# A fused attention and mixture-of-experts kernel: GpSimd's subtraction in two pieces, one group of routing operations a step later, a lower bound on one column at a time

## The chip, the cores and the metric

One core of a Trainium2 chip runs the whole program. The engines are TensorE (PE, with its weight loads PEld), VectorE (DVE), ScalarE (ACT), GpSimd (POOL) and SyncE (SP, which here issues most DMAs). The metric is device time in microseconds, the median of repeated runs.

## The reference, cut to what matters

```python
def _attn_ref(q, kv, w_sr):                      # B=4, C=128, q: 4 x 12288 x 128
    kv_pool = kv.reshape(B, H // r, r, W // r, r, C).mean(axis=(2, 4))
    k = v = kv_pool.reshape(B, -1, C) @ w_sr     # 768 keys per batch
    s = scale * (q @ k.transpose(0, 2, 1))
    a = np.exp(s - s.max(-1, keepdims=True))
    a /= a.sum(-1, keepdims=True) + 1e-09
    return a @ v
def _moe_ref(x, w_gate, w_output_gate, w1, w2):  # 8 experts, 49152 tokens x 128, hidden 1024
    logits = x @ w_gate
    e_idx = np.argmax(logits, axis=1)
    probs = np.exp(logits - logits.max(-1, keepdims=True))
    probs /= probs.sum(-1, keepdims=True) + 1e-09
    gate_w = probs[np.arange(N), e_idx]
    eom = 1.0 / (1.0 + np.exp(-(x @ w_output_gate)))
    ...
        h = np.maximum(x[mask] @ w1[e], 0.0)
        out[mask] = gate_w[mask, None] * eom[mask, e, None] * (h @ w2[e])
```

## The kernel before, in words

Values of 32 bits are carried as two halves of 16 bits, a high one (rounded) and a low one (the rest), and a product is three matmuls: high by high, high by low, low by high.

The queries are cut into 96 groups of 512 tokens (index `i`), each into four blocks of 128 (index `j`). The main loop runs over `i` and eight steps `s`; every second step starts a block. For each block, `qk` makes the scores S (six matmuls of 384 columns, L483 to L487) and DVE their negative maximum `nm` (L489, L490). `qk_exp` lets ACT write the probabilities `pr`, 768 columns of float32 (L504), and afterwards lets DVE scale a finished piece of output `o` (L825). `qk_round` lets ACT write the high half of the probabilities into `ph` (L517), and POOL the low half, `pr` minus the high half (L518). A DMA of SP transposes `ph` into `PT`. `pr` has two buffers, `ph` three.

A group later, `pv` multiplies PT with the values (18 matmuls, L540) into U, whose halves ACT (L544) and DVE (L545) write; two groups later, `moe_h` and `moe_y` push it through the one expert picked for the batch from the mean of its keys: per slice of the hidden layer three matmuls H (L790 to L792), the high half HH by ACT (L795), the low half HL by DVE (L796), and four slices later three matmuls Y (L805 to L807). PE's order is written out by hand, so PE stops where an operand is late.

Every four groups make a unit, and `routing` finds each token's expert, gate and place in the lists of tokens that go elsewhere. It is a Python generator whose pieces, between its `yield`s, are issued one or two per step between the work above; nearly all run on DVE on small tiles: L611 to L617; L620 to L626; L630 to L637 (`oh`, one where a token's expert is); then `se` (L656) and the output gate of the chosen expert, `zz` = gates times choice, summed to `z` and scaled (L658 to L661); the exponential of `z` (L663, ACT); the count of tokens `cnt` (L667), for which two small matmuls must have run; L669 to L676; L681; L684 to L687; L690 to L696. Then POOL scatters the rows to the lists by 16 indirect DMAs (L705). The last units are marked `ending`; there nothing is moved.

Beside this, each batch's keys and values are prepared during the batch before: POOL adds the pooled rows (L296 to L300), PE transposes them (L304), and `largest` (L170, L171) bounds the maximum found by DVE from below, for keys (`ve`) and for weights (`wm`, two columns).

`LAG` is 2: groups 0 and 1 run before the expert's work begins. The order within one engine is the order in which these calls are made.

Of the kernel before, what the change touches and what calls it, by code (L numbers as in the profile page):

```python
# [26 lines left out]
ALU = mybir.AluOpType  # L27
# [3 lines left out]
ts = bass.ts  # L31
# [6 lines left out]
NK = 768  # L38
# [11 lines left out]
LAG = 2  # L50
# [4 lines left out]
class Cfg:  # L55
# [24 lines left out]
    WA = ((6, 0, (0, 0)), (9, 0, (1, 0, 0)), (11, 0, (2, 0, 0), (1, 0, 1)), (13, 0, (2, 0, 1), (0, 1)),  # L80
          (16, 0, (1, 1, 0)), (18, 0, (2, 1, 0), (1, 1, 1)), (20, 0, (2, 1, 1)))
    PRB = 2
    QL, QT, QN = 0, 3, 6
    QLA = ((7,), (7,)) + ((0, 3, 6),) * 6
    QP1 = 5
# [15 lines left out]
def body(ctx, tc, q, kv, w_sr, w_gate, w_og, w1, w2, out, cfg=Cfg):  # L101
    nc = tc.nc
    pe, act, dve, pool, sp = nc.tensor, nc.scalar, nc.vector, nc.gpsimd, nc.sync
# [64 lines left out]
    def largest(m, ps):  # L168

        dve.tensor_reduce(out=m, in_=ps, op=ALU.max, axis=AX.X)  # L170
        dve.scalar_tensor_tensor(m, m, 2.0 ** -100, m, op0=ALU.max, op1=ALU.max)  # L171

    def powers(lo, inv, m):

# [10 lines left out]
    gps = psH.tile([P, GT], F32, tag="H", name="gps")  # L185
    pe.transpose(gps[:, 0:P], gmb, ident)
    largest(g3[:, 1:2], gps[:, 0:P])
    powers(g3[:, 2:3], g3[:, 3:4], g3[:, 1:2])
    dve.memset(wgB, 0.0)
# [41 lines left out]
    def kv_prep(b, fast):  # L231
# [99 lines left out]
        if fast:  # L331
            mean()
            choice(ps[:, 1, 0:E])
            next(QP[1])
            warm(cfg.WM[1])
        largest(e2[:, 5:6], ps[:, 0, 0:P])
        powers(e2[:, 0:1], e2[:, 1:2], e2[:, 5:6])
        dve.tensor_scalar(e2[:, 2:3], e2[:, 1:2], 2.0 ** 14, None, op0=ALU.mult)
# [159 lines left out]
    def qk_exp(i, j):  # L498

        S, nm, es, scale = QX.pop((i, j))  # L500
        c, g = unit[i]
        pr = wk.tile([P, NK], F32, tag="pr", bufs=cfg.PRB, name=f"pr{i}_{j}")
        bl = g * GB + j
# [6 lines left out]
    def qk_round(i, j):  # L510

        pr = PR.pop((i, j))
        ph = wk.tile([P, 2, NK], F16, tag="ph", bufs=3, name=f"ph{i}_{j}")
        if j in cfg.PHD and i < LAG:
            dve.tensor_copy(ph[:, 0, :], pr)
        else:
            act.activation(ph[:, 0, :], pr, AF.Copy)  # L517
        pool.tensor_tensor(ph[:, 1, :], pr, ph[:, 0, :], op=ALU.subtract)  # L518
        PH[(i, j)] = (ph, None, now[0])


# [72 lines left out]
    def routing(c):  # L594
# [8 lines left out]
        def T(nm, n=1, dt=F32, bufs=1):  # L603
            return rt.tile([P, CB * n], dt, tag=nm, bufs=bufs, name=f"{nm}{c}")[:, 0:nb * n]

        def T3(nm, n=E, bufs=1):
            return T(nm, n, F32, bufs).rearrange("p (b e) -> p b e", e=n)
# [38 lines left out]
        ending = g0 + ng + 2 >= NG  # L646
# [7 lines left out]
            hooks.append((now[0] + 1, counts))  # L654
        se = T("se")
        dve.tensor_reduce(out=se, in_=dn, op=ALU.add, axis=AX.X)  # L656
        zz = T3("dn")
        dve.tensor_tensor(zz, L[:, :, E:2 * E], oh, op=ALU.mult)  # L658
        z = T("z")
# [20 lines left out]
        x = T("x0", E)  # L680
# [44 lines left out]
    def w_split(b, t):  # L725
# [25 lines left out]
        if b:  # L751
            hooks.append((T, turn))
            while not ps:
                yield
            yield
            largest(m[:, 0:2], ps[0][:, :, 384:512])
        else:
            yield from until(0)
            wps = psY.tile([P, GT], F32, tag="Y", name="wmp")
            for n in range(2):  # L760
                pe.transpose(wps[:, ts(n, P)], mb[:, n, :], ident)
            largest(m[:, 0:2], wps[:, 0:2 * P].rearrange("p (n x) -> p n x", n=2))
# [223 lines left out]
    with tc.manual_schedule(engines={pool.engine, sp.engine, pe.engine, act.engine, dve.engine}):  # L986
# [30 lines left out]
        def k0(i):  # L1017
            return cfg.KV0[min(i // GPB, 1)]
# [6 lines left out]
        def after_values(ri, rc):  # L1025
            if rc is not None:
                logits(rc)

                def turn():
                    logits_turn(rc)  # L1030
                    rts.append([routing(rc), 0, rc])
                at(cfg.RG, turn)
            n = max(0, 8 * cfg.UD + cfg.UDS * ri - now[0])
            at(cfg.UT + n, u_turn, ri)
            at(cfg.UO + n, u_out, ri)
# [34 lines left out]
        for i in range(NG + OL):  # L1070
# [5 lines left out]
            for s in range(8):  # L1076
# [11 lines left out]
                for o in cfg.ORD if mi >= 0 else cfg.ORDA:  # L1088
# [4 lines left out]
                    if o == "s" and att and s % 2 == 0:  # L1093
                        qk(i, s // 2)
                        while late:
                            qk_round(*late.pop(0))
                    if o == "x" and att and s % 2 == 0:
                        qk_exp(i, s // 2)
                    if o == "r" and att and s % 2:
                        if s // 2 in cfg.PHD and i < LAG:  # L1100
                            late.append((i, s // 2))
                        else:
                            qk_round(i, s // 2)
# [7 lines left out]
                    if o == "u":  # L1111
                        for d, h in cfg.PVA:
                            x = i - d // 8
# [35 lines left out]
                if att and s == cfg.QL:  # L1149
                    n = min(ql + 2, i + cfg.QN + 1, NG)  # L1150
# [7 lines left out]
                if kp:  # L1158
                    n = (8 * (i % GPB - k0(i)) + s) % cfg.KVP[min(i // GPB, 1)]
# [25 lines left out]
        while events:  # L1185
            i, s = divmod(min(events), 8)
# [39 lines left out]
```

## Time and profile before

| | |
|---|---|
| median of 3 runs | 1962.98 us (1962.57 to 1963.02) |
| the profiled execution's own time | 1944.66 us |
| its span, first to last instruction | 1942.9 us |
| busy: PE, DVE, ACT, POOL | 96%, 77%, 68%, 60% |
| mean granted PE clock | 0.993 |

Busy shares are averages over the span. A busy PE is shown with modelled ends: its matmuls overlap, so a wait of PE is shown shorter than it is.

### The profile page before, as it was taken

What the parts mean: (1) busy time and instruction counts of PE and PEld (TensorE: products, weight loads), DVE (VectorE), ACT (ScalarE), POOL (GpSimd) and SP (SyncE); (2) the same over time, 40 slices, a digit from 0 to 9 for tenths busy, and PEclk for the clock granted to TensorE, in tenths of its full rate; (3) what the DMA queues carried; (4) which work ended last, traced back from release to release, by engine and by line L of the source; (5) the groups of instructions that cost most, each with busy time, mean ns of one, the idle gap of its engine ahead of it and who ended that gap; (6) DMA issues with size and microseconds to landing.
All of it is one profiled execution on the core that took longest, in us unless ns stands there. A gap on an engine that the chain in (4) does not pass through costs nothing. (4 is left out here: it accounts for less than half of the span.)

```text
span 1942.9 us, 31028 instructions
## 1 busy us (share of the span) xinstructions
PE 1870.8 (96%) x10225; PEld 951.0 (49%) x10225; DVE 1504.7 (77%) x3005; ACT 1321.3 (68%) x2391; POOL 1159.8 (60%) x996
## 2 busy tenths in 40 slices
PE   6999999999999999999999999999999999999997
PEld 4444455454445544545444554444445555545544
DVE  6776877888878778788787787787877877877773
ACT  3767767676776766676767776667677767767653
POOL 2537566564675676754756656656466456466462
PEclk9999999999999999999999999999999999999999
DMA  8877788788988887878788988778778778786642
GB/s 234 161 153 160 168 163 180 153 163 169 183 170 165 170 178 159 168 145 187 141 168 172 187 174 169 162 155 151 167 148 167 152 147 166 154 159 142 133 105 70
DMA packets 884017, 311.63 MB, mean 160 GB/s; under 512 B 827584, under 2 KB 833857, under 8 KB 883856
## 3 DMA queue, kind: packets, MB, share of 16 engines
q1 hardware_dynamic: 870944, 309.18, 78.7%
q0 software_dynamic: 12480, 0.40, 0.5%
q8 instruction: 81, 1.33, 0.3%
q14 instruction: 80, 0.66, 0.1%
q10 hardware_dynamic: 432, 0.07, 0.0%
HBM read 56.83 MB, written 51.25 MB: 56 GB/s over the span
## 5 line engine op out<-in xcount | busy, mean ns | idle before, releaser
L518 POOL TENSOR_TENSOR ph<-pr,ph 128x768 f16<-128x768 f32 x384 | 633.0, 1649 | 629.5 <-ACT ph L517 383.2
L796 DVE SCALAR_TENSOR_TENSOR HL<-H,HH 128x512 f16<-128x512 f32 x768 | 526.0, 686 | 142.3 <-ACT HH L795 127.9
L795 ACT ACTIVATE HH<-H 128x512 f16<-128x512 f32 x768 | 456.5, 594 | 246.6 <-PE H L792 240.3
L504 ACT ACTIVATE pr<-S,nm,qm 128x768 f32<-128x768 f32 x384 | 381.0, 992 | 240.2 <-DVE nm L490 222.7
L705 POOL DMA_INDIRECT scr<-rw,idx x384 | 383.1, 998 | 95.8 <-issue 88.1
L489 DVE TENSOR_REDUCE nm<-S 128x1 f32<-128x768 f32 x384 | 365.3, 951 | 86.8 <-PE S L487 86.3
L540 PE MATMUL U<-PT,V 128*128 128x512 f16 (+1 forms) x1746 | 406.1, 378 | 7.4 <-DVE HL L796 5.1
L517 ACT ACTIVATE ph<-pr 128x768 f16<-128x768 f32 x380 | 319.9, 842 | 2.4 <-DMA PT<-ph 1.9
L790 PE MATMUL H<-U,w 128*128 128x512 f16 x768 | 292.3, 381 | 12.3 <-DVE HL L796 7.0
L791 PE MATMUL H<-U,w 128*128 128x512 f16 x768 | 292.1, 380 | 0.0
L807 PE MATMUL Y<-HL,w 128*128 128x512 f16 x768 | 291.3, 379 | 0.7 <-DVE HL L796 0.6
L792 PE MATMUL H<-U,w 128*128 128x512 f16 x768 | 291.7, 380 | 0.0
L805 PE MATMUL Y<-HH,w 128*128 128x512 f16 x768 | 291.4, 379 | 0.3 <-ACT ys L810 0.3
L806 PE MATMUL Y<-HH,w 128*128 128x512 f16 x768 | 291.3, 379 | 0.0
L540 PEld LDWEIGHTS <-V 128*128 128x128 f16 x1746 | 171.4, 98 | 212.6 <-issue 11.5
L483 PE MATMUL S<-K,qT 128*128 128x384 f16 x768 | 189.2, 328 | 13.1 <-ACT pr L504 7.5
L487 PE MATMUL S<-K,qT 128*128 128x384 f16 x768 | 189.0, 328 | 1.3 <-DVE qT L459 1.0
L485 PE MATMUL S<-K,qT 128*128 128x384 f16 x768 | 188.9, 328 | 0.5 <-DVE K L349 0.5
L825 DVE TENSOR_TENSOR o<-S,msw 128x256 f32<-128x256 f32 x176 | 74.8, 425 | 89.0 <-ACT pr L504 87.6
L792 PEld LDWEIGHTS <-w 128*128 128x128 f16 x768 | 75.3, 98 | 91.4 <-issue 1.4
L807 PEld LDWEIGHTS <-w 128*128 128x128 f16 x768 | 75.2, 98 | 90.8 <-issue 0.3
L805 PEld LDWEIGHTS <-w 128*128 128x128 f16 x768 | 75.2, 98 | 88.3 <-issue 0.5
(209 smaller groups left out, 1865.4 us busy)
## 6 DMA issues: line engine op xcount, KB each, us to landing
kvs<-in_kv_dram SPq DMA_DIRECT2D x96, 256.0 KB
q<-in_q_dram SPq DMA_DIRECT2D x96, 256.0 KB
urows<-uT SPq DMA_DIRECT2D x96, 256.0 KB
out_dram<-o SPq DMA_DIRECT2D x96, 256.0 KB
PT<-ph SPq DMA_TRANSPOSE x384
scr<-rw,idx POOLq DMA_INDIRECT x384
wr<-in_moe_w_dram SPq DMA_DIRECT2D x8, 512.0 KB
tw<-in_moe_w_dram SPq DMA_DIRECT2D x4, 512.0 KB
```

The lines of the kernel that those rows point to most:

```text
L489: dve.tensor_reduce(out=nm[:, 0:1], in_=S[:, :, 0:384], op=ALU.max, axis=AX.XY, negate=True)
L504: act.activation(pr.rearrange("p (a k) -> p a k", a=2), S[:, :, 0:384], AF.Exp, bias=nm[:, 1:2], scale=es, accum_out=SUMS[c][:, bl:bl + 1])
L517: act.activation(ph[:, 0, :], pr, AF.Copy)
L518: pool.tensor_tensor(ph[:, 1, :], pr, ph[:, 0, :], op=ALU.subtract)
L540: pe.matmul(PVP[i][:, cols], ops[n][0], ops[n][1][:, cols], start=(n == 0), stop=(n == len(ops) - 1))
L705: ins = pool.indirect_dma_start(out=scr, out_offset=bass.IndirectOffsetOnAxis(ap=idx[:, bl:bl + 1], axis=0), in_=rw[:, bl, :], in_offset=None,
L790: pe.matmul(H, w1h[:, ts(f, P)], UH, start=True, stop=False)
L792: pe.matmul(H, w1l[:, ts(f, P)], UH, start=False, stop=True)
L795: act.activation(HH, H, AF.Relu)
L796: dve.scalar_tensor_tensor(HL, H, 0.0, HH, op0=ALU.max, op1=ALU.subtract)
L805: pe.matmul(Y, w2h[:, ts(f, P)], HH, start=(f == 0), stop=False)
L807: pe.matmul(Y, w2h[:, ts(f, P)], HL, start=False, stop=(f == NFB - 1))
```

## The change

Three edits. `qk_round`, from group 2 on, issues POOL's subtraction as two operations of 384 columns in place of one of 768. `routing` yields once more, between `se` and `zz`, except in the ending units. `largest` bounds each column of `m` by an operation with a constant (`tensor_scalar`), where one operation read `m` twice (`scalar_tensor_tensor`).

```diff
+    PLN = 2
...
         dve.tensor_reduce(out=m, in_=ps, op=ALU.max, axis=AX.X)
-        dve.scalar_tensor_tensor(m, m, 2.0 ** -100, m, op0=ALU.max, op1=ALU.max)
+        for n in range(m.shape[1]):
+            dve.tensor_scalar(m[:, n:n + 1], m[:, n:n + 1], 2.0 ** -100, None, op0=ALU.max)
...
             act.activation(ph[:, 0, :], pr, AF.Copy)
-        pool.tensor_tensor(ph[:, 1, :], pr, ph[:, 0, :], op=ALU.subtract)
+        for x in [slice(0, NK)] if i < LAG else [ts(h, NK // cfg.PLN) for h in range(cfg.PLN)]:
+            pool.tensor_tensor(ph[:, 1, x], pr[:, x], ph[:, 0, x], op=ALU.subtract)
...
         dve.tensor_reduce(out=se, in_=dn, op=ALU.add, axis=AX.X)
+        if not ending:
+            yield
         zz = T3("dn")
         dve.tensor_tensor(zz, L[:, :, E:2 * E], oh, op=ALU.mult)
```

On DVE, this is the order of the second unit's routing around the new `yield`, before (`dn` is the tile that `zz` lies in, `nm` the scores' maximum, `o` the output, `U` the low half of U):

```order
L656 TENSOR_REDUCE se_2285<-dn_2262 128x16
L658 TENSOR_TENSOR dn_2287<-L_2210,oh_2269 128x128
L660 TENSOR_REDUCE z_2289<-dn_2287 128x16
L661 TENSOR_TENSOR z_2289<-z_2289,rinv_2214 128x16
L489 TENSOR_REDUCE nm_3_2313<-S_3_2304 128x1
L490 TENSOR_SCALAR nm_3_2313<-nm_3_2313,qm_860 128x1
L796 SCALAR_TENSOR_TENSOR HL_4_2321<-H_4_2316,HH_4_2320 128x512
L825 TENSOR_TENSOR o_2229<-S_3_2304,msw_1468 128x256
L545 SCALAR_TENSOR_TENSOR U_2343<-U_2292,U_2343 128x512
L796 SCALAR_TENSOR_TENSOR HL_5_2353<-H_5_2348,HH_5_2352 128x512
L489 TENSOR_REDUCE nm_0_2375<-S_0_2366 128x1
```

And the same place of the changed kernel, whose lines are numbered a little higher:

```order
L659 TENSOR_REDUCE se_2317<-dn_2293 128x16
L491 TENSOR_REDUCE nm_3_2340<-S_3_2331 128x1
L492 TENSOR_SCALAR nm_3_2340<-nm_3_2340,qm_867 128x1
L801 SCALAR_TENSOR_TENSOR HL_4_2348<-H_4_2343,HH_4_2347 128x512
L830 TENSOR_TENSOR o_2260<-S_3_2331,msw_1524 128x256
L548 SCALAR_TENSOR_TENSOR U_2370<-U_2319,U_2370 128x512
L663 TENSOR_TENSOR dn_2374<-L_2240,oh_2300 128x128
L665 TENSOR_REDUCE z_2376<-dn_2374 128x16
L666 TENSOR_TENSOR z_2376<-z_2376,rinv_2244 128x16
L801 SCALAR_TENSOR_TENSOR HL_5_2384<-H_5_2379,HH_5_2383 128x512
L491 TENSOR_REDUCE nm_0_2407<-S_0_2398 128x1
```

The three operations of `zz` and `z` went from ahead of `nm`, HL, `o` and the low half of U to behind them, ahead of the next HL and `nm`; what follows (`cnt` and so on) keeps its place, since the generator waited a step for the count's matmuls anyway. Only in the first unit do later pieces shift too. ACT's exponential of `z` moves from behind U's high half to behind the next block's probabilities. PE's and SP's orders are the same in both kernels.

On POOL, five rows in the middle of the first batch, before (`scr` are the scatters):

```order
L518 TENSOR_TENSOR ph_2_2748<-pr_2_2729,ph_2_2748 128x768
L705 DMA scr<-rw_2583,idx_2578 394240x4 x2
L518 TENSOR_TENSOR ph_3_2819<-pr_3_2785,ph_3_2819 128x768
L705 DMA scr<-rw_2583,idx_2578 394240x4 x2
L518 TENSOR_TENSOR ph_0_2869<-pr_0_2849,ph_0_2869 128x768
```

And with the change:

```order
L521 TENSOR_TENSOR ph_2_2787<-pr_2_2768,ph_2_2787 128x384 x2
L710 DMA scr<-rw_2619,idx_2614 394240x4 x2
L521 TENSOR_TENSOR ph_3_2859<-pr_3_2825,ph_3_2859 128x384 x2
L710 DMA scr<-rw_2619,idx_2614 394240x4 x2
L521 TENSOR_TENSOR ph_0_2910<-pr_0_2890,ph_0_2910 128x384 x2
```

Each subtraction became two in a row (376 of the 384), with nothing of POOL between them; the order is otherwise kept, but for the first unit, where two additions and a scatter change places with their neighbours.

## Rows read from the trace of the kernel before

**Rows 1.** Steady stretch: us, busy of PE, PEld, DVE, ACT, POOL, clock, DMA.

```profile
150.00:1880.00 1730.00, 1695.81 (x9280) 854.40 (x9278) 1367.26 (x2674) 1209.41 (x2184) 1078.15 (x919) 1.00 0.82 162
```

**Rows 2.** Waits, whole run: waiting engine and line, releaser, us in total, times, longest.

```profile
PE H L790 <- DVE HL L796: 7.0, 12, 1.3
...
PE U L540 <- DVE HL L796: 5.1, 6, 1.7
...
PE H L790 <- DVE U L545: 4.7, 11, 1.0
...
ACT pr L504 <- POOL ph L518: 2.0, 4, 0.7
```

**Rows 3.** DVE by line, 150 to 1880 us: busy us, mean ns, idle before.

```profile
L658 DVE TENSOR_TENSOR dn<-L,oh 128x128 f32<-128x128 f32 (+1 forms) x23 | 34.1, 1482 | 0.8
...
L634 DVE TENSOR_TENSOR oh<-t,m 128x128 f32<-128x128 f32 (+1 forms) x23 | 8.6, 375 | 0.8
```

**Rows 4.** Timeline of the third unit's `zz`: start us, us, engine, line, [idle before].

```profile
283.02 2.11 PE L540 MATMUL U<-PT,V 128*128 128x512 f16 x9
...
283.82 1.63 POOL L518 TENSOR_TENSOR ph<-pr,ph 128x768 f16<-128x768 f32 x1 [3.66 <-ACT ph L517]
283.89 1.79 DVE L658 TENSOR_TENSOR dn<-L,oh 128x128 f32<-128x128 f32 x1
...
286.04 0.18 DVE L661 TENSOR_TENSOR z<-z,rinv 128x16 f32<-128x16 f32 x1
...
289.03 0.69 DVE L545 SCALAR_TENSOR_TENSOR U<-U,U 128x512 f16<-128x512 f32 x1
...
289.77 0.38 PE L790 MATMUL H<-U,w 128*128 128x512 f16 x1 [0.34 <-DVE U L545]
...
290.45 1.64 POOL L518 TENSOR_TENSOR ph<-pr,ph 128x768 f16<-128x768 f32 x1 [5.00 <-ACT ph L517]
```

**Rows 5.** PE busy from 2 to 7 us behind each L658, 22 stretches.

```profile
sum 110.00, PE 104.52; mean PE 4.75
```

**Rows 6.** Timeline around 533 us, POOL's operations back to back.

```profile
532.57 1.07 DVE L684 SCALAR_TENSOR_TENSOR st<-cnt,ebase 128x8 f32<-128x8 f32 x1
...
533.57 1.26 POOL L296 TENSOR_TENSOR kvs<-kvs 128x512 f32<-128x512 f32 x1
```

**Rows 7.** PE busy in six stretches at other routing pieces, from 371 to 1005 us.

```profile
sum 30.00, PE 24.63; mean PE 4.10
```

**Rows 8.** Timeline around 1400 us: a bound of two columns.

```profile
1397.64 1.38 DVE L171 SCALAR_TENSOR_TENSOR wm<-wm 128x2 f32<-128x2 f32 x1
```

**Rows 9.** PE busy, 932 to 938 and 1397.6 to 1403.6 us, behind such bounds.

```profile
sum 12.00, PE 8.82; mean PE 4.41
```

**Rows 10.** Timeline around 448 us.

```profile
447.56 1.64 POOL L518 TENSOR_TENSOR ph<-pr,ph 128x768 f16<-128x768 f32 x1 [1.86 <-ACT ph L517]
...
447.98 0.15 DVE L265 TENSOR_SCALAR chi<-ch 128x1 int32<-128x1 f32 x1
```

**Rows 11.** Two stretches, columns as in rows 1.

```profile
771.00:775.00 4.00, 1.15 (x6) 0.39 (x5) 2.79 (x5) 3.28 (x9) 2.35 (x3) 1.00 0.85 202
775.00:778.50 3.50, 3.50 (x11) 1.87 (x12) 0.92 (x1) 1.91 (x4) 3.12 (x3) 0.51 0.99 213
```

**Rows 12.** POOL by line and shape, whole run, columns as in rows 3.

```profile
L518 POOL TENSOR_TENSOR ph<-pr,ph 128x768 f16<-128x768 f32 x384 | 633.0, 1649 | 629.5 <-ACT ph L517 383.2 <-issue 220.4 <-DVE ph L515 21.2
...
L778 POOL TENSOR_TENSOR w<-wr,w 128x512 f16<-128x512 f32 x16 | 18.6, 1164 | 1.1 <-ACT w L774 1.0
```

**Rows 13.** PE busy, 20 stretches of 4 us behind L690 to L696 (0.82 us).

```profile
sum 80.00, PE 77.45; mean PE 3.87
```

**Rows 14.** Timeline around 926 us: L692 beside a subtraction.

```profile
926.09 1.64 POOL L518 TENSOR_TENSOR ph<-pr,ph 128x768 f16<-128x768 f32 x1 [4.79 <-issue]
926.18 1.59 DVE L692 SCALAR_TENSOR_TENSOR idx<-sel,ix 128x16 int32<-128x16 f32 x1
...
929.87 0.38 PE L790 MATMUL H<-U,w 128*128 128x512 f16 x1 [1.28 <-DVE HL L796]
```

## The prediction

> **What bounds the kernel now.** I read the busy time of the steady stretch first, then who waits for whom, then the timeline around a few of those waits. In the stretch from 150 to 1880 us PE is busy for 1695.8 of 1730 us at full clock, while DVE is idle for a fifth of it and POOL for more than a third [rows 1]. PE bounds it; only the 34 us in which PE waits can be won, and somewhat more, since a matmul of 512 columns is shown 0.38 us long and started every (2.11 - 0.38) / 8 = 0.216 us [rows 4]: each wait is really 0.16 us longer than shown. PE waits mostly for DVE: 16.8 us in 29 waits for HL and for the low half of U [rows 2].
>
> Why is DVE late, with so much idle time? `zz` (L658) takes 1482 ns on average; `oh` (L634), the same shape with two operands from SBUF, takes 375 ns [rows 3]. The timeline shows the reason: POOL's subtraction began at 283.82, `zz` at 283.89, and `zz` ended at 285.68, 0.23 us behind the subtraction's end [rows 4]. L684, of 8 columns, was held the same way, and so was the bound L171, of two [rows 6, 8]. A DVE operation with two inputs from SBUF that starts while POOL computes stands still until POOL's operation ends; I call it caught. Not every operation is: HL reads one input from PSUM, and `tensor_scalar` on one column took its usual 0.15 us in the middle of a subtraction [rows 10]. Behind a caught operation all of DVE's queue is late (`nm`, HL, `o`, U), then ACT, then PE: at 289.77 PE waited for U, whose DVE part had queued behind that `zz` [rows 4].
>
> **The change part by part.** The sum is made against the profiled execution (1944.7 us, of which 1942.9 are span); it lies 18.3 us below the median of the runs, 1963.0, and I take the same microseconds off the median.
>
> *`zz` a step later.* In 22 steady units `zz` starts beside a subtraction and loses 1.48 - 0.38 = 1.1 us, with everything of DVE behind it. In the five microseconds that begin 2 us after each, PE idles 110.0 - 104.5 = 5.5 us; these are some 20 waits, so really 5.5 + 20 x 0.16 = 8.7 us [rows 5]. Now `nm`, HL, `o` and U go first. The group stands behind U and ahead of the next HL; its other two operations ended 0.54 us behind `zz` (286.22 against 285.68, rows 4), so not caught it takes 0.38 + 0.54 = 0.92 us. L690 to L696 (0.82 us) stand in just such a place already, behind U: in 20 stretches behind them PE idles 2.55 us [rows 13], and 17 of the 20 show no idle time; the rest has the key transposition in it. So a group of this length is covered there by PE's queued matmuls. I take three quarters of the 8.7 as won, 6.5 us; bounds 0 and 8.7.
>
> Can it be caught again? `zz` itself starts with U's end, `z` times `rinv` (L661, two inputs from SBUF) 0.38 + 0.36 = 0.74 us after (286.04 against 285.68, rows 4). The next subtraction started 0.73 us after U's end (290.45 against 289.72, rows 4), and will start a little earlier, since ACT's exponential of `z` has left the place between. That is a dead heat. Caught by a piece, it loses at most the piece, 0.9 us, ahead of HL and `nm`. I put 1.0 us against all units; bounds 0 and, at the one wait of 1.28 + 0.16 us seen behind a caught operation in this very place [rows 14], 22 x 1.44 = 31.7.
>
> *Two pieces.* 768 columns take 1649 ns and 512 take 1164 [rows 12]: 1.9 ns a column and some 0.19 us fixed. A piece of 384 should take 0.92 us and a pair 1.84, so POOL works 376 x 0.19 = 73 us more. What hides it: POOL waits 383 us for ACT in front of this line alone [rows 12], and ACT waited for a subtraction to free `pr` only 4 times, 2.0 us in all [rows 2]. I cost it at nothing. If a piece took as long as 512 columns, the pair would take 2.33 us, 256 us more in all, still less than that idle time; without the cover each block would pay its 0.19 us, 73 us. What the pieces give: DVE is let in between POOL operations that stand back to back. L684 ended at 533.64 although POOL's next had begun at 533.57 [rows 6]. So a caught operation waits for the end of a piece, on average half as long. In six stretches where other routing pieces were caught PE idles 5.4 us, in 6 waits, really 6.3 [rows 7]. Half of it, 3.2 us; bounds 0 (some were caught by key additions of 512 columns, which stay whole) and 6.3.
>
> *The bound.* L171 was held for 1.38 us [rows 8]; two `tensor_scalar` on one column take 2 x 0.15 by the one that ran beside a subtraction [rows 10]. That is 1.1 us earlier for what queues behind it, twice where PE stopped: 12.0 - 8.8 = 3.2 us idle in four waits, really 3.8 [rows 9]. I take 3.0; bounds 0 and 3.8.
>
> A rule speaks against this edit. The Trainium skill's page "VectorE: DVE Perf Modes", section "The perf-mode tier table", gives fp32 `tensor_scalar` in SBUF a two-port mode, and its page "SBUF — State Buffer", section "SBUF: two separate sides", says that an operation in such a mode fights GpSimd for one port pair as one with two SBUF inputs does. By that the bound would be caught as before and the sum 3.0 us smaller. The rows on one column say otherwise, and I go by them.
>
> *The clock.* At 771 PE idles 2.85 us, then runs 3.4 us at a granted clock of 0.51, the lower of its two levels (1.2 GHz) [rows 11]. Much the same happens once more, at 1236 us. DVE's lateness from earlier caught pieces adds to both, and key preparation does too. I take 2.0 us of the some 9 that both cost (2 x 2.85 idle and 2 x 1.7 of clock); bounds 0 and 9.
>
> Sum: -6.5 + 1.0 - 3.2 - 3.0 - 2.0 = -13.7 us: 1931 for a profiled execution, 1949 for the median.
>
> **The rivals.**
>
> *Caught again.* `z` times `rinv` starts just behind the first piece in nearly all units. It loses some 0.7 us of DVE there, where `zz` lost 1.1 and cost PE 8.7 / 22 = 0.4 us a unit; at 0.3 a unit it gives back 6.6 us in place of the 1.0: 1955. For it: the dead heat. Against: L690 to L696 show room for 0.82 us there [rows 13].
>
> *All of it.* The waits that follow from caught operations vanish, the two falls of the clock too: 8.7 + 6.3 + 3.8 + 9 = 28: 1935. Against: the key preparation, which stays.
>
> *PE waits elsewhere.* DVE is on time, and ACT's chain (probabilities, then HH, then `ph`) ends as late as before: PE loses elsewhere most of what it wins, and 3 us remain: 1960. For it: ACT works for 1209 of 1730 us [rows 1] and has its own order. Against: ACT had waited for the late `nm`.
>
> *Slower: the second piece follows before DVE gets in.* A caught operation then waits for 1.84 us, more than the 1.65 before, and `z` times `rinv` is caught ahead of HL. With 1.44 us of PE as in [rows 14] in half of the units that is +15.8, with +1 for the other pieces, against -8.7 and -3.0: +5, 1968. It decides from about 8 caught units on. Against: L684 was let in between two operations [rows 6]. The same page "SBUF — State Buffer" of the Trainium skill says that whoever starts first holds the port pair for the whole instruction; it does not say who is next, and the trace agrees as far as it goes.
>
> **How the numbers follow.** The forecast 0.56 (its own range 1943 to 1957, from taking half or nearly all of each term), caught again 0.17, all of it 0.09, elsewhere 0.12, slower 0.06. Within 0.2% (4 us) is about what a measurement of this kernel cannot tell from no change, so slower starts at 1967. Faster gets nearly all of the first three, 0.79; same gets the fourth and the edges of its neighbours, 0.14; slower 0.07. The range reaches from the all-of-it case to the elsewhere case with its margin: 1935 to 1963.
>
> **What would show it.** Right: `zz` near 0.38 us on average and no idle time of PE from U's low half behind it; L684 near 0.5 us; the bounds at 0.15 us; pieces near 0.92 us and POOL some 70 us busier; PE idle in the steady stretch near 22 us instead of 34. Wrong: `z` times `rinv` near 1 us on average (caught again); DVE operations ending behind a second piece (not let in); ACT waiting for POOL at L504, or pieces above 1.2 us (the cover gone); or PE's idle time unchanged under other names.

## The result, and the profile after

The changed kernel took 1943.28 us (median of 4 runs, 1942.22 to 1944.98) beside 1962.83 for the kernel before (4 runs): 19.6 us less, a ratio of 0.9901 with a 95% interval of 0.9884 to 0.9918. In a later series, on another chip, the same pair took 1927.21 and 1942.17: 15.0 us less, 0.9925 (0.9911 to 0.9939). The forecast was 14 us less, 1949 beside 1963, a ratio of 0.9930: it lies inside the second interval and 0.0012 above the end of the first.

The profiled execution of after (1944.02 us, one of its timed runs) is only 0.6 us shorter than that of before (1944.66). Two rows of each timeline show why: ACT's copies of the expert's finished sums, `ys`, of group 3 and of group 91, groups 0 to 95 (columns: start us, us, engine, line). Before:

```profile
143.50 0.59 ACT L810 ACTIVATE ys<-Y 128x512 f32<-128x512 f32 x1
...
1879.50 0.59 ACT L810 ACTIVATE ys<-Y 128x512 f32<-128x512 f32 x1
```

After:

```profile
140.16 0.59 ACT L815 ACTIVATE ys<-Y 128x512 f32<-128x512 f32 x1
...
1865.75 0.59 ACT L815 ACTIVATE ys<-Y 128x512 f32<-128x512 f32 x1
```

After is 3.3 us ahead at group 3 and 13.75 at group 91. It loses nearly all of that again in the last groups. This is its timeline there:

```profile
1876.51 0.38 PE L797 MATMUL H<-U,w 128*128 128x512 f16 x1
...
1879.05 0.38 PE L797 MATMUL H<-U,w 128*128 128x512 f16 x1
...
1884.78 0.60 ACT L800 ACTIVATE HH<-H 128x512 f16<-128x512 f32 x1 [7.16 <-remote]
...
1888.35 0.60 ACT L800 ACTIVATE HH<-H 128x512 f16<-128x512 f32 x1 [2.96 <-remote]
...
1890.42 1.11 PE L842 MATMUL ot<-ident,ys 128*128 128x128 f32 x4 [10.99 <-ACT ys L815]
```

ACT writes the HH at 1888.35 from the H that PE had finished at 1876.89; in between ACT does almost nothing, and PE, which is at the end of its own queue, idles 10.99 us. The releaser is given as "remote": by the ends shown, nothing was late. The ends of matmuls are modelled, though, and the trace also records when the semaphore changed by which H tells ACT that it is done: here at 1884.76 and 1888.32, each 0.02 us ahead of an HH, and 9.2 and 11.4 us behind the ends shown for these two H. So ACT started when it was told; late was the signal, or the true end of the matmul. The experiments below say whether this stall belongs to the change.

In the steady stretch the rows answer to [rows 1 to 3]. First the busy times of 150 to 1860 us (columns as in [rows 1]; up to 1860, since the stall of after begins ahead of 1880), before and after:

```profile
150.00:1860.00 1710.00, 1676.12 (x9176) 844.72 (x9174) 1352.02 (x2626) 1201.20 (x2167) 1068.50 (x906) 1.00 0.82 163
```

```profile
150.00:1860.00 1710.00, 1682.06 (x9231) 850.25 (x9229) 1343.09 (x2651) 1211.67 (x2175) 1128.46 (x1270) 1.00 0.82 163
```

PE idles 27.9 us in place of 33.9. In the second traces of the two kernels, below, it is 24.4 and 37.9 us.

Then DVE by line in after, 150 to 1880 us (busy us, mean ns, idle before):

```profile
L440 DVE SCALAR_TENSOR_TENSOR q<-q,qm,q 128x512 f16<-128x512 f32 x87 | 81.2, 934 | 0.0
...
L666 DVE TENSOR_TENSOR z<-z,rinv 128x16 f32<-128x16 f32 (+2 forms) x24 | 11.4, 475 | 0.8
...
L663 DVE TENSOR_TENSOR dn<-L,oh 128x128 f32<-128x128 f32 (+2 forms) x24 | 9.2, 383 | 0.1
...
L689 DVE SCALAR_TENSOR_TENSOR st<-cnt,ebase 128x8 f32<-128x8 f32 x24 | 8.1, 337 | 0.0
```

`zz`, now L663, takes 383 ns where it took 1482 [rows 3]: caught in one unit only (0.82 us at 207 us), no longer in all 22. `z` times `rinv` (L666) takes 475, far above the 0.18 us of one that is not caught [rows 4]: caught in part of the units. L684, now L689, takes 0.34 us. The waits of PE and ACT in after, whole run (total us, times, longest):

```profile
PE H L795 <- DVE HL L801: 4.9, 6, 1.3
...
PE S L485 <- DVE cnt L672: 3.4, 2, 2.1
...
PE U L543 <- DVE HL L801: 2.5, 4, 1.2
...
ACT pr L506 <- POOL ph L521: 2.3, 4, 1.0
...
PE H L795 <- DVE U L548: 1.3, 2, 1.0
```

PE's waits for HL and U's low half fell from 16.8 us in 29 [rows 2] to 8.7 us in 12, and ACT waits for a subtraction as seldom as before.

### The profile page after: what moved, and what is told of

Same layout as the page of the kernel before. It is cut to its first block, busy times and chain, and to the rows that moved or that the text cites. A ratio compares the mean times of both kernels' runs of the same rounds, so it can differ in the third digit from the quotient of the medians.

```text
span 1942.3 us, 31545 instructions
## 1 busy us (share of the span) xinstructions
PE 1867.1 (96%) x10225; PEld 952.2 (49%) x10225; DVE 1485.9 (76%) x3009; ACT 1328.2 (68%) x2391; POOL 1216.9 (63%) x1372
## 5 line engine op out<-in xcount | busy, mean ns | idle before, releaser
L521 POOL TENSOR_TENSOR ph<-pr,ph 128x384 f16<-128x384 f32 (+1 forms) x760 | 686.0, 926 | 559.2 <-issue 440.0
L710 POOL DMA_INDIRECT scr<-rw,idx x384 | 387.8, 1010 | 94.9 <-issue 90.9
```

The lines of the kernel that those rows point to most:

```text
L521: pool.tensor_tensor(ph[:, 1, x], pr[:, x], ph[:, 0, x], op=ALU.subtract)
L710: ins = pool.indirect_dma_start(out=scr, out_offset=bass.IndirectOffsetOnAxis(ap=idx[:, bl:bl + 1], axis=0), in_=rw[:, bl, :], in_offset=None,
```

## The experiments

**The kernel before again, and each edit alone (four kernels beside each other).** The first is unchanged:

> The kernel before, unchanged. The profiled execution of before (1944.7 us) was 18.3 us shorter than its timed runs (1962.8), while the one of after (1944.0 us) is one of its timed runs, and 13.6 us of it are one stall of PE at 1877 to 1890 us, where before shows none. Theory A: the stall near the end comes and goes from run to run or from kernel to kernel, whatever the three edits do; then this trace shows a stall of 10 us or more near the end and its time is 1958 to 1963 us, or it shows none and the time is near 1945. Theory B: the 18.3 us of before are spread over the steady stretch (PE idle there 45 us or more in place of 34); then the change wins in its timed runs more than the traces show.

It took 1959.63 us against 1959.59. Its group 91 stands here:

```profile
1883.34 0.59 ACT L810 ACTIVATE ys<-Y 128x512 f32<-128x512 f32 x1
```

That is 3.8 us behind the first trace of before, and from there to the end of the span it takes 1957.9 - 1883.3 = 74.6 us where the first trace took 1942.9 - 1879.5 = 63.4. Together 15.0 us, all of the difference between the two executions (1959.64 - 1944.66). The 11.2 us lie where after has its stall: HH starts at 1900.82 for an H that is shown to end at 1893.18 (its signal stands at 1900.80), and PE idles 8.6 us. So theory A holds: this stall is no work of the change; before has it too, in an execution as long as its timed runs. Theory B falls: PE idles 37.9 us in 150 to 1860, not 45.

The step alone:

```diff
         dve.tensor_reduce(out=se, in_=dn, op=ALU.add, axis=AX.X)
+        if not ending:
+            yield
         zz = T3("dn")
```

> Before with the one yield between se and zz and nothing else. Prediction's step: zz is no longer caught, minus 6.5 us (0 to 8.7), and z times rinv caught in some units gives back 1.0 (0 to 6.6), so 1955 to 1958 us. Rival, pieces carry the gain: z times rinv is caught by the whole subtraction of 1.65 us in about half of the units and nothing is won, 1962 us. Rival, the gain is the end stall only: 1943 to 1946 or 1962, and nothing in between.

It took 1951.94 us, ratio 0.9964 (0.9951 to 0.9977): by the ratio 7 us less (4.5 to 9.6). The expected 1955 to 1958, meant from 1963, are 5 to 8 less, so this fits. The five microseconds at `zz`'s old place, 2 to 7 us behind the end of `se`, in 22 units as in [rows 5] (which had 5.48 us idle), now show 0.43:

```profile
sum 110.00, PE 109.57 PEld 54.33 DVE 93.17 ACT 66.95 POOL 42.95; mean PE 4.98 PEld 2.47 DVE 4.24 ACT 3.04 POOL 1.95
```

`z` times `rinv` is caught by the whole subtraction in 11 of 22 units, 842 ns on average, and still nearly all of the gain stays. The rival "nothing is won" fell.

The pieces alone:

```diff
-        pool.tensor_tensor(ph[:, 1, :], pr, ph[:, 0, :], op=ALU.subtract)
+        for x in [slice(0, NK)] if i < LAG else [ts(h, NK // cfg.PLN) for h in range(cfg.PLN)]:
+            pool.tensor_tensor(ph[:, 1, x], pr[:, x], ph[:, 0, x], op=ALU.subtract)
```

> Before with the subtraction in two pieces and nothing else. Prediction's step: caught operations wait half as long, minus 3.2 us for the other pieces (0 to 6.3) and some 0.5 to 0.7 us of each zz, 22 units, another 4: 1955 to 1960 us; zz falls from 1.48 to about 0.9 us. Rival, the second piece follows before DVE gets in: zz rises to 1.8 us or more and the time is 1963 to 1970. Rival, the end stall only: 1943 to 1946 or 1962, nothing in between.

It took 1950.23 us, ratio 0.9956 (0.9943 to 0.9969), by the ratio 8.6 us less, where 3 to 8 were expected. `zz` takes 750 ns and is caught in every unit as before, but by a piece:

```profile
L660 DVE TENSOR_TENSOR dn<-L,oh 128x128 f32<-128x128 f32 (+2 forms) x24 | 18.0, 750 | 0.8
```

At its place PE now idles 110.0 - 107.4 = 2.6 us in place of 5.48:

```profile
sum 110.00, PE 107.40 PEld 52.63 DVE 91.85 ACT 79.78 POOL 29.20; mean PE 4.88 PEld 2.39 DVE 4.17 ACT 3.63 POOL 1.33
```

So at this place the pieces alone take half of what the step takes.

The bounds alone:

```diff
-        dve.scalar_tensor_tensor(m, m, 2.0 ** -100, m, op0=ALU.max, op1=ALU.max)
+        for n in range(m.shape[1]):
+            dve.tensor_scalar(m[:, n:n + 1], m[:, n:n + 1], 2.0 ** -100, None, op0=ALU.max)
```

> Before with the two or one one-column bounds and nothing else. Prediction's step: minus 3.0 us (0 to 3.8), 1959 to 1963 us, each bound 0.15 us. Rival, by the rule that two-port modes fight for the port too: the bounds that meet a subtraction take 1 us or more and the time does not change, 1963. Rival, the end stall only: 1943 to 1946 or 1962, nothing in between.

It took 1956.15 us, ratio 0.9988 (0.9980 to 0.9997): by the ratio 2.3 us less, between 0.6 and 3.9. The timeline shows a pair of bounds that starts 0.27 us into a whole subtraction and takes 0.21 us:

```profile
1395.00 1.63 POOL L519 TENSOR_TENSOR ph<-pr,ph 128x768 f16<-128x768 f32 x1 [1.47 <-ACT ph L518]
1395.27 0.21 DVE L172 TENSOR_SCALAR wm<-wm 128x1 f32<-128x1 f32 x2
```

The rival, taken from a rule, falls with that. None of the three times lies at 1943 to 1946 or at 1962, as the rival of all three had it, so the end stall does not carry the gain either.

**After again, without the step, with four pieces, and with ACT's stream shifted (four kernels on another chip, before 1942.17 us there).**

> The kernel after, unchanged, beside the kernel before on one chip, to stand next to the parts. If the parts add up (0.36, 0.44 and 0.12 per cent alone), 0.991 of before or 18 us less; if the step and the pieces win the same waits twice, the parts alone would give more than the whole and the ratio would be 0.993 to 0.994. The stall near the end, in ACT's HH of slices 731 to 733 and 743 to 746, which all traces show but the first of before, should be there again with 12 to 14 us.

Measured 1927.21 us, 0.9925 (0.9911 to 0.9939), between the two expectations. The stall was not there. The timeline shows HH behind H at once, and the transposition `ot` without a wait:

```profile
1872.13 0.38 PE L797 MATMUL H<-U,w 128*128 128x512 f16 x1
...
1872.54 0.60 ACT L800 ACTIVATE HH<-H 128x512 f16<-128x512 f32 x1 [0.70 <-PE H L797]
...
1873.84 0.66 PE L842 MATMUL ot<-ident,ys 128*128 128x128 f32 x4
```

Group 91 stands at 1861.38, and from there it takes 63.3 us, as in the first trace of before. The stall thus comes with the series a kernel is run in, not with the kernel: 11 to 13 us in after and in the four kernels above, where before took 1963 and 1960 us beside them, none in this trace, where it took 1942. By these times the runs of before have it where those of the other kernel have it, so it should cancel in each ratio; the runs without a trace cannot show it.

The yield taken out of after:

```diff
         dve.tensor_reduce(out=se, in_=dn, op=ALU.add, axis=AX.X)
-        if not ending:
-            yield
         zz = T3("dn")
```

> After without the yield: pieces and bounds. With pieces alone zz was still caught 23 times but for 0.42 us in place of 1.16, and the waits of PE in the 5 us behind it fell from 11.2 to 4.0 us. Theory, overlap: the step can only win those 4.0, less 1.5 that z times rinv gives back ahead of the count's wait, so this kernel is 2 to 4 us slower than after. Rival, additive: the step is worth its 7.7 us also beside the pieces; this kernel is 6 to 8 us slower than after.

Measured 1928.91 us, 0.9929 (0.9915 to 0.9942): 1.7 us slower than after by the medians and 0.8 by the ratios, which the runs do not tell from nothing; the additive rival, 6 to 8, falls. Alone the step won 7 us, beside the pieces 1 or 2 (up to 3 by the spread of the six runs of each). So they win, for the most part, the same waits.

Four pieces:

```diff
-    PLN = 2
+    PLN = 4
```

> After with four pieces of 192 columns in place of two of 384. A piece should take 0.19 + 192 x 0.0019 = 0.55 us, four 2.2 us, POOL 143 us more busy than in after. Theory, a caught operation waits for the end of the piece that it meets: z times rinv loses 0.3 us in place of 0.65, all caught operations of DVE together some 40 us in place of 53, and PE wins 1 to 4 us, 1940 to 1943. Rival, the cover is gone: ACT waits for POOL at the probabilities and the low halves come late, slower than after by 2 us or more. Rival, PE covers what is left of the catches: the same as after within 1 us.

Measured 1921.95 us, 0.9896 (0.9880 to 0.9912): 5.3 us faster than after, a little more than the 1 to 4 expected. The reason given was only half right. `z` times `rinv` fell to 316 ns on average, but all catches of DVE together did not shrink: L440 rose from 934 to 1064 ns, though the pieces are shorter.

```profile
L440 DVE SCALAR_TENSOR_TENSOR q<-q,qm,q 128x512 f16<-128x512 f32 x87 | 92.6, 1064 | 0.0
```

PE's waits for HL and U's low half are 5.4 us there, where the trace of after beside it has 9.6, and PE runs one stretch at the lower clock in the steady stretch where after has two; what each of these is worth is not separated. POOL's row, with a piece of 0.56 us, gives 1504 x 0.561 = 844 us by the means, and 789 us busy, as back-to-back pieces overlap a little:

```profile
L521 POOL TENSOR_TENSOR ph<-pr,ph 128x192 f16<-128x192 f32 x1504 | 789.3, 561 | 412.5 <-issue 335.1 <-ACT ph L519 70.4 <-POOL ph L521 2.1
```

ACT's copies ahead of everything:

```diff
+        dm = cst.tile([P, 64], F32, name="dm")
+        dve.memset(dm[:, 0:1], 0.0)
+        for n in range(1, 41):
+            act.activation(dm[:, n:n + 1], dm[:, 0:1], AF.Copy)
         ld, vprep = kv_load(0, True), kv_prep(0, True)
```

> After with 40 small copies on ACT ahead of everything, where ACT idles until 10 us (plus one memset on DVE). It asks what the stall near the end is tied to: ACT ran HH of slices 731 to 733 and 743 to 746 of the hidden layer 2 to 11 us after its operands were there, the same slices in five traces. Theory, ACT's place in its instruction stream: the stall moves some 40 instructions forward, to slices of about 705 to 722, or goes, and the time changes by several us up to 13. Rival, tied to the work there (the scatters of the last units, what ACT waits for): the same slices, the same 12 to 14 us, the time of after within 2 us.

Measured 1926.71 us, the time of after within 0.5. Since no kernel of this series had the stall, it says nothing about its cause: inconclusive.

**Going on: is the step needed, do other pieces help, and how small is too small (three kernels beside each other, before 1943.82 us).** Four pieces without the yield:

> Four pieces and the bounds, without the yield (after has two pieces, the bounds and the yield). If pieces and step win the same waits, zz caught by a piece of 0.55 us loses 0.2 to 0.3 us only and the step has nothing left to win: the ratio to before is that of four pieces with the step, 0.9896, within 0.001. Rival, the step is worth something of its own (2 us or more beside two pieces, the interval of the runs left that open): 0.9905 to 0.992.

Measured 1922.36 us, 0.9898 (0.9883 to 0.9912): the same as four pieces with the step, so the step has nothing left to win there that these runs can tell (some 4 us between two series). `zz` is then caught in its old place but takes 432 ns, 0.06 more than uncaught:

```profile
L661 DVE TENSOR_TENSOR dn<-L,oh 128x128 f32<-128x128 f32 (+2 forms) x24 | 10.4, 432 | 0.8
```

Four pieces with the other long operations of POOL halved (on top of the edit above):

```diff
-                pool.tensor_tensor(x[:, 0, :], x[:, 0, :], v, op=ALU.add)
+                for p in (slice(0, 256), slice(256, 512)):
+                    pool.tensor_tensor(x[:, 0, p], x[:, 0, p], v[:, p], op=ALU.add)
...
-            pool.tensor_tensor(ws[n][:, 1, ts(x, 512)], t[:, n, ts(x, 512)], ws[n][:, 0, ts(x, 512)], op=ALU.subtract)
+            for p in (2 * x, 2 * x + 1):
+                pool.tensor_tensor(ws[n][:, 1, ts(p, 256)], t[:, n, ts(p, 256)], ws[n][:, 0, ts(p, 256)], op=ALU.subtract)
```

> Four pieces with the step and the bounds, and the other long operations of POOL in two pieces too: the key additions (54 of 512 columns, 1.30 us) and the low halves of the weights (16, 1.16 us), 0.7 us each piece. Theory, what is caught waits for the end of the operation that it meets, so the catches by these (0.5 to 1.2 us, some 20 in a run) halve and PE wins 1 to 3 us more: 0.988 to 0.989 of before. Rival, PE does not wait behind these catches any more: 0.9896 as with four pieces alone.

Measured 1917.15 us, 0.9869 (0.9855 to 0.9884), the fastest of all: 26.7 us below before, 5.2 below four pieces without the yield in the same series, and more than the theory's 0.988 to 0.989. The rival falls; that the halved operations catch less was not looked at by itself. PE is idle for 20.2 us of 150 to 1860, where before idled 33.9:

```profile
150.00:1860.00 1710.00, 1689.79 (x9299) 855.93 (x9297) 1351.25 (x2702) 1218.01 (x2186) 1251.85 (x2056) 1.00 0.82 164
```

Six pieces:

```diff
-    PLN = 2
+    PLN = 6
```

> Six pieces of 128 columns with the step and the bounds. A piece takes 0.19 + 0.24 = 0.43 us, six 2.6 us, POOL some 1500 us busy. Theory, shorter catches still win: z times rinv loses below 0.25 us and the ratio is 0.988 to 0.989. Rival, the cover is gone: the low half of the probabilities is ready 0.75 us later than with two pieces, ACT waits for pr and PE for PT or ACT, and the ratio rises to 0.991 or more. Rival, the optimum is flat: 0.9896 within 0.001.

Measured 1936.46 us, 0.9967 (0.9955 to 0.9979): by the ratios 8 us worse than two pieces and 14 worse than four. No one wait carries that: PE idles 29.4 us in 150 to 1860, where with four pieces it idles 22.6, and it runs three stretches at the lower clock, where with four pieces it runs one. The cover is gone in part. ACT now waits for a subtraction 13 times, with 8.8 us in all:

```profile
ACT pr L506 <- POOL ph L521: 8.8, 13, 2.1
```

And DVE is at times shut out for longer. A `sume` of 16 columns, in the timeline, began beside a scatter and was held through eleven of the twelve pieces of two blocks: it ended at 584.31, 0.03 us behind the end of the eleventh, while the twelfth ran on to 584.67:

```profile
579.79 4.52 DVE L619 SCALAR_TENSOR_TENSOR sume<-SUM,ve 128x16 f32<-128x16 f32 x1
580.02 4.65 POOL L521 TENSOR_TENSOR ph<-pr,ph 128x128 f16<-128x128 f32 x12
...
585.20 1.02 PE L543 MATMUL U<-PT,V 128*128 128x512 f16 x4 [0.89 <-DVE HL L801]
```

**The step and the bounds without pieces:**

```diff
-    PLN = 2
+    PLN = 1
```

> After with the subtraction whole: the step and the bounds only. It prices the pieces beside the step, which the prediction put at 3.2 us (0 to 6.3). By the prediction this kernel is 3 us slower than after, 0.994 to 0.9945 of before if after is 0.9925. Rival, by the parts alone: the step (0.9964) and the bounds (0.9988) add to 0.995, and as z times rinv is caught in 11 units for 1.4 us in place of 0.65, the pieces are worth 5 to 7 us also beside the step: 0.995 to 0.996.

Measured 1929.59 us beside 1943.90, 0.9938 (0.9925 to 0.9952): 14.3 us below before by the medians, where after was 15.0 below; by the ratios 0.0013 x 1943 = 2.5 us slower than after, with some 4 us of uncertainty, as two series are compared. The prediction's price fits and the rival's of 5 to 7 us less well, but a worth of nothing is not excluded.

## Why the prediction was right, step by step

**The mechanism** held. A DVE operation with two inputs from SBUF stands until POOL's operation ends: `zz` took 1482, 750 and 432 ns in its old place beside subtractions of 768, 384 and 192 columns.

**`zz` moved, -6.5 of at most 8.7.** In after the old place shows 110.0 - 109.4 = 0.6 us idle, against 5.48 [rows 5]; with 0.16 us for each of some 18 waits that went, that is 4.9 + 2.9 = 7.8 us won (1.5 more by the second trace of before, which idles 6.95 us there).

```profile
sum 110.00, PE 109.38 PEld 54.34 DVE 92.82 ACT 68.81 POOL 45.37; mean PE 4.97 PEld 2.47 DVE 4.22 ACT 3.13 POOL 2.06
```

The three quarters that I took were too few, but in the bounds.

**`z` times `rinv` caught again, +1.0.** The dead heat came to pass. In the third unit the two started 0.01 us apart:

```profile
282.34 0.69 DVE L548 SCALAR_TENSOR_TENSOR U<-U,U 128x512 f16<-128x512 f32 x1
282.95 0.37 DVE L663 TENSOR_TENSOR dn<-L,oh 128x128 f32<-128x128 f32 x1
283.66 1.78 POOL L521 TENSOR_TENSOR ph<-pr,ph 128x384 f16<-128x384 f32 x2 [2.40 <-issue]
283.67 0.93 DVE L666 TENSOR_TENSOR z<-z,rinv 128x16 f32<-128x16 f32 x1
284.52 0.68 DVE L801 SCALAR_TENSOR_TENSOR HL<-H,HH 128x512 f16<-128x512 f32 x1
```

L666 ended at 284.60, while the pair of pieces ran until 285.44: let in between the two. It was caught in 11 of 22 units, as many as half of them, and loses (475 - 180) x 24 = 7.1 us of DVE. PE feels it in two places only, of 22 stretches of 5 us behind L663:

```profile
818.84:823.84 5.00, 3.70 (x19) 1.61 (x16) 4.80 (x12) 2.77 (x7) 1.78 (x2) 1.00 0.54 101
...
1280.21:1285.21 5.00, 2.97 (x15) 1.22 (x12) 4.80 (x12) 2.66 (x7) 1.78 (x2) 1.00 0.57 106
...
sum 110.00, PE 106.67 PEld 53.08 DVE 101.60 ACT 73.89 POOL 45.91; mean PE 4.85 PEld 2.41 DVE 4.62 ACT 3.36 POOL 2.09
```

All 3.33 us of idle time stand in these two, where PE waits for `cnt`. That wait was there before:

```profile
PE S L483 <- DVE cnt L667: 2.8, 2, 1.7
```

In after it is 3.4 us, as the row above shows, so 0.6 us are given back, not the 6.6 of the rival "caught again". With the subtraction whole (the kernel without pieces) it is 4.3.

**Two pieces, -3.2.** A piece takes 918 ns, as estimated (0.92), a pair 1.78, since the second starts some 0.05 us ahead of the first's end in the record. POOL's row, as in [rows 12]:

```profile
L521 POOL TENSOR_TENSOR ph<-pr,ph 128x384 f16<-128x384 f32 x752 | 672.9, 918 | 532.6 <-issue 440.0 <-ACT ph L519 88.6 <-POOL w L783 0.6
```

POOL works 60 us more in 150 to 1860 us (1128 against 1068), less than the 73 predicted, and the cover held. Worth beside the step: 2.5 us by the ratios and 0.7 by the medians, within some 4. But this term has no one value: alone the pieces won 8.6, since they halve what the step removes. That I priced them on what the step leaves was right; had both been priced alone, as 7 and 8.6, the sum would have counted some 5 us twice. That rests on the kernel without the yield: the 19.6 us of the first series by themselves would fit a plain sum of the parts, 17.9, as well.

The reason "DVE is let in between" was right for small operations and wrong for one: L440, 512 columns, was held over both pieces in each of the 9 cases in which it met a first piece of a pair.

```profile
161.89 1.79 POOL L521 TENSOR_TENSOR ph<-pr,ph 128x384 f16<-128x384 f32 x2
...
162.32 1.92 DVE L440 SCALAR_TENSOR_TENSOR q<-q,qm,q 128x512 f16<-128x512 f32 x1
```

It ended at 164.24, 0.56 us behind the pair. So the rival "the second piece follows before DVE gets in" has its case, and with it a sign of being wrong that the prediction named. It did not decide the time: all 87 together lose 934 - 839 = 95 ns each more than before, 8 us of DVE, and PE's waits for DVE fell all the same.

**The bound, -3.0.** Measured alone 2.3 (0.6 to 3.9). All 13 bounds in after take 144 to 155 ns. The prediction set against this term a rule of the Trainium skill ("VectorE: DVE Perf Modes", section "The perf-mode tier table", with "SBUF — State Buffer"), by which the bound would be caught; the trace disagrees for one column, at 0.21 us for two of them 0.27 us into a subtraction. The first page's own section "Mode 2×_2P — use both read ports for one tensor" asks that the outermost non-unit dimension be even, or odd and equal for source and destination. One column has no such dimension, and the section does not say what holds then. So the tier table alone was too short a reading; the trace decides.

**The clock, -2.0: the term that failed.** In after, PE still idles ahead of the probabilities at 767 and then runs at the lower clock level, where before did so at 775 [rows 11]:

```profile
763.10:767.10 4.00, 1.51 (x8) 0.45 (x5) 2.85 (x5) 3.28 (x8) 2.49 (x4) 0.97 0.83 192
766.90:770.40 3.50, 3.28 (x11) 1.66 (x12) 0.64 (x1) 2.16 (x6) 3.18 (x4) 0.52 0.98 198
```

The idle time in front of it is as long as before (2.67 us more than a matmul's distance, in both), and no operation of DVE is held in the six microseconds ahead of it: it is not made by caught pieces. That the key preparation makes it was not tested. At 1229 the wait stayed too, without a fall; another fall followed the longer `cnt` wait at 1285. The second trace of after has its two falls at 1225 and 1283 and none at 767. In all, this term won nothing: two stretches of 3.4 us at the lower level in both traces of before and in both of after. It was there to be won in other kernels: the traces show one such stretch with four pieces, none with four pieces without the yield or with all long operations halved, and three with six pieces, at 1.7 us each.

**A sign that did not come.** The prediction wanted PE's idle time in the steady stretch near 22 us instead of 34. It is 28 and 24 in the two traces of after, of 150 to 1860 us, against 34 and 38 in the two of before: down by some 10 us, as forecast, but not to 22.

**What was not in the sum.** The first 150 us: after is 3.3 us ahead at group 3 (3.0 in the other trace of after, but before's two traces are 1.8 apart there themselves). The bounds and the first unit's `zz` act there as well, and the prediction summed over 150 to 1880 us alone. With -7.8, +0.6, -2.5, -2.3 and some -2 for this, one comes to -14: the 13.75 us at group 91 and the 15.0 of the second series. The agreement is in part luck: the 2 us of the clock that did not come were made up by some 2 us of the first 150 us, which the sum did not have. Nor do the traces carry it to the tenth: between groups 3 and 91 the two traces of before are 5.7 us apart, and those of after 4.7. Why the first series shows 19.6 is not settled; the two intervals overlap (16.1 to 17.3 us less).

**The offset to the median.** I took 18.3 us as a constant between a profiled execution and the runs, without a reason. By the second trace of before, 11.2 us of it are the stall near the end and 3.8 lie ahead of it; no trace shows the other 3.3. To carry it over came out right because both kernels had the stall in that series, which I could not know. To compare the two profiled spans would have been wrong: they differ by 0.6 us.

## What to carry to other kernels

Two edits that shorten the same wait are not added up: price the second on what the first leaves, and test each alone and without. Where a helper engine shuts out another for the length of an operation, cut its long operations and time several cuts, since shorter is not always better: here four pieces of 0.56 us, with the other long ones halved too, gave 26.7 us, two pieces 15, and six pieces 7, each against before in its own series. And before two profiled executions are compared, align them at the same piece of work along the run; spans alone hid the whole gain here.

## What the hardware showed that was not expected

DVE does not always get in between POOL operations that stand back to back. With two pieces most small operations were let in at the first end, while L440 was not; with six pieces a `sume` of 16 columns waited through eleven (4.52 us). The Trainium skill's page "SBUF — State Buffer", section "SBUF: two separate sides", says that whoever starts first holds the port pair for its whole instruction; that covers one wait and not those behind it. What decides who is next is not settled; it is not the size alone, with 16 columns in the one case and 512 in the other.

ACT started HH 8 to 12 us after the end shown for its H, at the same slices near the end (744 to 746 of 768), in the traces of after and of the first four experiments, and in none of the other eight nor in the first trace of before. The semaphore records put the delay between PE's H and its signal, not in ACT: with the stall the signal stands 0.02 us ahead of the HH, elsewhere 0.01 to 0.02 us behind the end of the H. The same five traces also lack about a tenth of these records all along the run (73 to 78 of 768 H have none within 0.03 us of their end; in the other nine traces 0 to 3), so something differed in these series beyond the last groups. No transfer or code load in the trace explains it, and the test that should have told ACT's place in its stream from the work there fell into a series without it. Its cause is open.
